# The second layer's first product as seven block products, tokens in two halves

## The chip, the cores and the metric

The kernel runs on one core of a Trainium2 chip. A core has five engines with queues of their own: TensorE (PE; its weight loads are listed apart as PEld), VectorE (DVE), ScalarE (ACT), GpSimd (POOL) and SyncE (SP, which here issues DMAs). Each engine works through its queue in program order and waits on semaphores for the others. SBUF is the working memory with 128 partitions; PSUM, eight banks of 128 x 512 float32, is where TensorE writes. The metric is the device time of one execution in microseconds (us).

## The reference

Three stages follow each other: clustered attention, a layer of eight experts of which each token takes one, and a layer of eight experts of which each token takes all, with weights from a balanced routing. The change lies in the third.

```python
def _moe2_ref(x, w_gate, w1, w2):            # x 1536 x 512, w1 8 x 512 x 1024, w2 8 x 1024 x 512
    logits = x @ w_gate
    logits = logits - logits.max()
    P = np.exp(logits)
    for _ in range(8):
        P /= P.sum(1, keepdims=True) + 1e-09
        P /= P.sum(0, keepdims=True) + 1e-09
        P *= N / E
    for e in range(E):
        h = np.maximum(x @ w1[e], 0.0)
        out += P[:, e:e + 1] * (h @ w2[e])
```

## The kernel before

All float32 products are made from two parts: a value rounded to the matmul's reduced format (`wh`, `xth`, `hh`; dtype fp32r) and the rest (`wl`, `xtl`, `hl`). A product of two such operands takes three matmuls: high by high, high by low, low by high. PSUM sums them.

Class `Weights` (L349 to L420) streams both layers' weights in chunks of 512 KB: 256 columns of `w1`, then the matching 256 rows of `w2`. `load` (L375) has SP issue the transfers into a ring of three raw buffers `wr`. `split` (L396 to L400) has ACT round a chunk into `wh` (L398) and DVE subtract to get `wl` (L399), then asks for later chunks. The parts stand in twelve slots. `get` keeps the split stream a fixed number of chunks ahead of use (`upto`).

First layer (loops at L821 on): per expert `e`, 256 token rows; per quarter `c` of the hidden dimension, `up` (L776 on) makes 24 matmuls of 256 columns into `hp` (L784), ACT and DVE make `hh` (L788) and `hl` (L789); `down` (L793 on) makes 12 matmuls of 512 columns into `acc` (L799), one quarter behind. After the last quarter, ACT and DVE copy `acc` to `y` (L802, L803) and SP writes it to the DRAM array `ys` (L808). `load2` (L723) reads 512 rows of `ys` back into `acc_o`; SP has to wait for the write to land first. `gated` (L729) multiplies a tile of 128 rows by its gate on DVE, and `rows` transposes it on TensorE (L738), after which ACT and DVE make `xth` and `xtl` (L740, L741). In the kernel before, `gated(0)` is issued eight quarters after its `load2`, four tiles are transposed at the end of the first layer, the other eight inside the second.

Second layer (loops at L957 on): per expert, three groups `g` of 512 tokens; per group eight slices `f` of 128 hidden columns. `up2` (L917 on) makes 12 matmuls of 512 columns into `hp` (L923), ACT makes `hh` (L926), DVE `hl` (L927). `down2` (L933 on) makes 12 matmuls of 512 columns into four `acc` banks (L937), one slice behind. After the eighth slice DVE scales `acc` by the routing weight `pm` and adds it to `acc_o` (L947); at the last expert POOL writes the rows out by an indirect DMA (L950). The second layer's routing, `balance` (L867 on), is threaded into the first slices: 24 matmuls for the logits (L877), then a chain of small DVE operations and small matmuls (L908).

The order on TensorE, ACT and DVE is that of the program text (a manual schedule); SP runs the DMA issues in one queue.

## Time and profile before

| | us |
|---|---|
| median of three runs | 1584.37 |
| lowest, highest | 1583.82, 1586.54 |
| span of the profiled execution | 1582.6 |
| TensorE busy in it | 1544.8 |
| DVE, ACT, POOL busy | 649.3, 497.7, 173.2 |
| second layer's first matmul starts at (timeline) | 497.60 |

The span runs from the first to the last instruction. The profiled execution's own device time is not listed apart from its span; the median of the runs is 1.8 us above the span, and that is taken for what lies around it. A matmul's listed duration overlaps the next one's, so what one costs is read from the distance of two starts, not from its duration.

### The profile page before, as it was taken

Reading aid. Unit: us, or ns where it says so; the run is one execution under the profiler, and the core shown is the slowest. Engines: PE = TensorE matmul, PEld = TensorE weight load, DVE = VectorE, ACT = ScalarE, POOL = GpSimd, SP = SyncE. Lnnn points to the kernel's source line nnn. Section 1 sums busy time; section 2 is a strip of 40 time slices with the busy share of each in tenths; the row PEclk is TensorE's granted clock in tenths of the full one; section 3 lists DMA queues with packets and bytes.
Section 4 is the critical chain, followed back from the end, with each engine's and each line's share of the span. In section 5 each row is a group of like instructions: output and inputs, shape, how many; then the busy total and the mean of one; then the engine's idle time right before and its main releaser. Section 6 shows DMA issues by size and latency. Waiting matters only on the chain.

```text
span 1582.6 us, 19864 instructions
## 1 busy us (share of the span) xinstructions
PE 1544.8 (98%) x7998; PEld 1306.0 (83%) x7998; DVE 649.3 (41%) x1109; ACT 497.7 (31%) x841; POOL 173.2 (11%) x205
## 2 busy tenths in 40 slices
PE   6999999799999999999999999999999999999998
PEld 5998999689998778888888888888888888888886
DVE  5888888556665225222411222231231132122111
ACT  3887778555554212211211211211121121111110
POOL 3254464132100000000000000000000000000000
PEclk9999999899999999999999999999999999999999
DMA  5575563286766001100200210120020021000000
GB/s 147 126 184 152 144 172 91 54 265 218 259 216 200 1 1 52 55 0 14 93 0 1 67 40 1 40 67 1 14 86 9 0 67 41 0 14 1 27 27 27
DMA packets 86591, 117.64 MB, mean 74 GB/s; under 512 B 20760, under 2 KB 55576, under 8 KB 86496
## 3 DMA queue, kind: packets, MB, share of 16 engines
q1 hardware_dynamic: 83216, 108.97, 23.5%
q0 software_dynamic: 2752, 7.36, 1.4%
q8 instruction: 64, 1.05, 0.3%
q14 instruction: 31, 0.25, 0.1%
q10 hardware_dynamic: 528, 0.02, 0.0%
HBM read 83.98 MB, written 10.51 MB: 60 GB/s over the span
## 4 chain that ended last, share of the span: by engine, by line
PE 76%; issue 2%; DMA 1%; DVE 1%; ACT 0%; POOL 0%; POOLq 0%; ACTq 0%
PE hp L923 33%; PE acc L937 32%; PE hp L784 5%; PE acc L799 5%; DMA wr<-w1a 1%; PE tp L771 0%; PE tp L877 0%; PE tp L738 0%; DVE wl L399 0%; DMA wr<-w2a 0%; ACT wh L398 0%; DMA xg<-xd,inv_i 0%; POOL out L950 0%; PE tp L908 0%; DVE hl L789 0%
## 5 line engine op out<-in xcount | busy, mean ns | idle before, releaser
L927 DVE SCALAR_TENSOR_TENSOR hl<-hp,hh 128x512 fp32r<-128x512 f32 x192 | 132.7, 691 | 743.6 <-ACT hh L926 743.5
L926 ACT ACTIVATE hh<-hp 128x512 fp32r<-128x512 f32 x192 | 115.0, 599 | 858.6 <-PE hp L923 858.6
L923 PE MATMUL hp<-xth,wh 128*128 128x512 f32 x768 | 305.4, 398 | 0.0
L923 PE MATMUL hp<-xth,wl 128*128 128x512 f32 x768 | 303.0, 394 | 0.0
L923 PE MATMUL hp<-xtl,wh 128*128 128x512 f32 x768 | 302.5, 394 | 0.0
L937 PE MATMUL acc<-wh,hh 128*128 128x512 f32 x768 | 301.7, 393 | 0.0
L937 PE MATMUL acc<-wl,hh 128*128 128x512 f32 x768 | 300.3, 391 | 0.0
L937 PE MATMUL acc<-wh,hl 128*128 128x512 f32 x768 | 300.0, 391 | 0.0
L923 PEld LDWEIGHTS hp<-xth,wl 128*128 128x128 f32 x768 | 144.1, 188 | 35.0
L937 PEld LDWEIGHTS acc<-wh,hl 128*128 128x128 f32 x768 | 144.2, 188 | 33.2 <-DVE hl L927 0.4
L937 PEld LDWEIGHTS acc<-wh,hh 128*128 128x128 f32 x768 | 144.2, 188 | 32.9 <-ACT hh L926 0.4
L923 PEld LDWEIGHTS hp<-xth,wh 128*128 128x128 f32 x768 | 144.3, 188 | 32.5
L923 PEld LDWEIGHTS hp<-xtl,wh 128*128 128x128 f32 x768 | 144.3, 188 | 32.4
L937 PEld LDWEIGHTS acc<-wl,hh 128*128 128x128 f32 x768 | 144.2, 188 | 32.2
L399 DVE TENSOR_TENSOR wl<-wr,wh 128x1024 fp32r<-128x1024 f32 x120 | 142.3, 1222 | 49.8 <-ACT wh L398 48.8
L398 ACT CAST wh<-wr 128x1024 fp32r<-128x1024 f32 x120 | 121.5, 1049 | 40.8 <-PE acc L799 20.4
L950 POOL DMA_INDIRECT out<-acc,tok x12 | 11.7, 975 | 1105.5 <-DVE acc L947 1068.1
L265 DVE TENSOR_TENSOR pl<-pst,ph 128x512 fp32r<-128x512 f32 x144 | 95.3, 680 | 12.1 <-ACT ph L261 12.1
L221 DVE TENSOR_REDUCE nm<-sp 128x1 f32<-128x768 f32 x96 | 91.0, 949 | 15.9 <-PE sp L212 15.2
L231 ACT ACTIVATE e<-sp,nm 128x768 f32<-128x768 f32 x96 | 86.9, 905 | 26.0 <-DVE nm L221 25.6
L261 ACT CAST ph<-pst 128x512 fp32r<-128x512 f32 x144 | 83.7, 585 | 26.3 <-PE pst L247 13.8
L277 PE MATMUL ov<-ph,v 128*128 128x256 f32 x288 | 80.6, 306 | 0.1
(213 smaller groups left out, 1865.4 us busy)
## 6 DMA issues: line engine op xcount, KB each, us to landing
wr<-w1a SPq DMA_DIRECT2D x32, 512.0 KB, 4.2
wr<-w2a SPq DMA_DIRECT2D x32, 512.0 KB, 4.5
wr<-w1b SPq DMA_DIRECT2D x32, 512.0 KB, 3.4
wr<-w2b SPq DMA_DIRECT2D x32, 512.0 KB, 4.2
q<-hh SPq DMA_DIRECT2D x32, 192.0 KB, 3.2
k<-hh SPq DMA_DIRECT2D x32, 192.0 KB, 3.6
ys<-y SPq DMA_DIRECT2D x8, 514.0 KB, 4.0
acc<-ys SPq DMA_DIRECT2D x3, 1028.0 KB, 7.0
```

The costliest lines, as they stand in the source:

```text
L221: nc.vector.tensor_reduce(out=nm, in_=sp[:, :, :384], axis=AX.XY, op=ALU.max, negate=True)
L231: nc.scalar.activation(out=e, in_=sp[:, :, :384], func=AF.Exp, bias=nm, accum_out=st["rs", t // 2][:, t % 2 : t % 2 + 1])
L261: nc.scalar.copy(out=w[3](w[1]), in_=w[0])
L265: nc.vector.tensor_tensor(out=w[3](w[2]), in0=w[0], in1=w[3](w[1].bitcast(F32)), op=ALU.subtract)
L277: nc.tensor.matmul(ov[:, :256], st["v2"][:, kt, :], w[:, kt, :], start=kt == 0 and i == 0, stop=kt == 5 and i == 1)
L398: self.nc.scalar.copy(out=wh, in_=r)
L399: self.nc.vector.tensor_tensor(out=wl, in0=r, in1=wh.bitcast(F32), op=ALU.subtract)
L784: nc.tensor.matmul(hp[:, f, :], w[:, kc, fs], xx[:, kc, :], start=kc == 0 and i == 0, stop=kc == 3 and i == 2)
L923: nc.tensor.matmul(hp, w[:, kc, fs], xx[:, kc, :], start=kc == 0 and i == 0, stop=kc == 3 and i == 2)
L926: nc.scalar.activation(out=hh, in_=hp, func=AF.Relu)
L927: nc.vector.scalar_tensor_tensor(out=hl, in0=hp, scalar=0.0, in1=hh.bitcast(F32), op0=ALU.max, op1=ALU.subtract)
L937: nc.tensor.matmul(acc[t], hx[:, as_], w[:, f % 2, :], start=f == 0 and i == 0, stop=f == 7 and i == 2)
```

## The change

The `w1` product of the second layer is made with seven block products in place of eight (Strassen, in Winograd's form). Tokens stand in two halves of 768. The work is cut in 64 items: half `s`, expert `e`, quarter `j` of the hidden dimension. In an item, x (768 tokens by 512) and `w1` (512 by 256) are cut 2 x 2; each block product is six matmuls of 384 columns, seven of them in an item make 42. The partial sums go through DVE (five additions), ACT (one copy, four roundings with relu) and DVE again (four low parts). The two PSUM banks `u0`, `u1` serve the seven groups in turn, and parts of the item before (`fill`, the 36 matmuls of 512 columns of its `w2` product) stand between the groups.

Weights are streamed once for each half. Each item's `w1` chunk is split twice: the chunk itself (`bh`, `bl`, of which three blocks are used) and, after four block subtractions in place, the four sums (`th`, `tl`). Slots go from twelve to nine, and `get` in the first layer runs 7 chunks ahead in place of 10. The block sums of the first half of x are built at the end of the first layer (`build_first`), those of the second half by POOL (item 8) and by ACT and DVE (item 31). `load2` reads six tiles after expert 4 and two tiles after experts 5, 6 and 7; ten of twelve tiles are gated and transposed in the first layer by a plan, and x keeps no split copy besides the block operands. The logits become 48 float32 matmuls of 8 columns with x as weights.

The core of the diff (renames, the same code moved, and the blocks' bookkeeping are cut):

```diff
 class Weights:
-    NA, NB = 8, 4
+    NS = 9
+        for _ in range(2):
             for e in range(8):
+                for j in range(4):
+                    self.src.append(w1b[e, j])
+                    self.src.append(w2b[e, j])
...
+    def build(self):
+        r = self.take()
+        th, tl = self.pair([128, 4, 256])
+        bh, bl = self.pair([128, 4, 256])
...
+        A.copy(out=bh, in_=r)
+        yield
+        for a in ((slice(0, 2), slice(0, 128)), (slice(2, 4), slice(0, 256))):
+            s_ = (slice(None),) + a
+            V.tensor_tensor(out=bl[s_], in0=r[s_], in1=bh.bitcast(F32)[s_], op=ALU.subtract)
+        yield
+        diff((0, 0), (0, 1), (0, 0))
+        diff((0, 1), (1, 1), (0, 1))
+        diff((1, 1), (1, 1), (0, 0))
+        diff((1, 0), (1, 0), (1, 1))
+        yield
+        A.copy(out=th, in_=r)
+        yield
+        V.tensor_tensor(out=tl, in0=r, in1=th.bitcast(F32), op=ALU.subtract)
+        self.load(3)
+        r = self.take()
+        wh, wl = self.pair([128, 2, 512])
+        A.copy(out=wh, in_=r)
+        yield
+        V.tensor_tensor(out=wl, in0=r, in1=wh.bitcast(F32), op=ALU.subtract)
+        self.load(3)
...
         def up(e, c, x):
-            wh, wl = W.get(0, e, c, 0, 2 * c + (8 if e == 0 else 10))
+            wh, wl = W.get(e, c, 0, 2 * c + 7)
...
-                if e in (3, 5):
-                    load2((e - 3) // 2)
+                if e == 4:
+                    load2(0, 6)
+                elif e > 4:
+                    load2(2 * e - 4, 2)
...
+        plan = {
+            (5, 1): "g0 g1", (5, 2): "r0 g2 r1 g3", (5, 3): "r2 g4 r3 g5 l0", (6, 0): "r4 r5 l2", (6, 1): "l4 g6 g7",
+            (6, 2): "r6 r7 x", (6, 3): "l6 x", (7, 0): "x x", (7, 1): "x g8 g9 w w", (7, 2): "x r8 r9 w w w", (7, 3): "l8 w",
+        }
...
+    GROUPS = (("a11", "b11", 0, True), ("s2", "t2", 1, True), ("a12", "b21", 0, False), ("s3", "t3", 1, False),
+              ("s1", "t1", 0, True), ("a22", "t4", 1, False), ("s4", "b22", 0, False))
...
+    def up2(k, fill, cuts, hooks):
+        wb = W.build() if k < 63 else iter(())
+        for g, (xn, wn, b, start) in enumerate(GROUPS):
+            for kc in range(2):
+                for i, (ww, xx) in enumerate(((wh, xh), (wh, xl), (wl, xh))):
+                    nc.tensor.matmul(p[:, N], ww[:, kc, :], xx[:, kc, :], start=start and kc == 0 and i == 0,
+                                     stop=kc == 1 and i == 2, skip_group_check=not start)
+            now = None
+            if g == 0:
+                r1 = new("r1")
+                nc.scalar.copy(out=r1, in_=p[:, N])
+            elif g == 1:
+                u2 = new("u2")
+                add(u2, r1, p)
+            elif g == 2:
+                nc.scalar.activation(out=parts("c11")[0], in_=p[:, N], func=AF.Relu)
+                lo("c11", p[:, N])
+            elif g == 3:
+                u3 = new("u3")
+                add(u3, r1, p)
+            else:
+                n, r = (("c22", u3), ("c21", r1), ("c12", u2))[g - 4]
+                c = new("cc", 2)
+                add(c, r, p)
+                nc.scalar.activation(out=parts(n)[0], in_=c, func=AF.Relu)
+                now = n, c
+            for f in hooks.get(g, ()):
+                f()
+            if g != 2:
+                next(wb, None)
+            if now:
+                lo(*now)
+            for f in fill[cuts[g] : cuts[g + 1]]:
+                f()
...
+    EVEN = [0, 5, 10, 15, 20, 25, 30, 36]
+    for k in range(64):
+        s, e, j = k // 32, k // 4 % 8, k % 4
+        cuts = EVEN
+        if k == 0:
+            cuts = [0, 12, 24, 24, 24, 24, 24, 24]
...
+        h = up2(k, fill, cuts, hooks)
+        fill = down2(s, e, j, h, acc, (3, 4, 5, 0, 1, 2) if k == 63 else None)
+    for f in fill:
+        f()
```

## Rows read from the trace of the kernel before

**Rows 1.** The page: busy us, share of the span and instructions by engine.

```profile
PE 1544.8 (98%) x7998; PEld 1306.0 (83%) x7998; DVE 649.3 (41%) x1109; ACT 497.7 (31%) x841; POOL 173.2 (11%) x205
```

**Rows 2.** The page's chain that ended last, shares of the span by line.

```profile
PE hp L923 33%; PE acc L937 32%; PE hp L784 5%; PE acc L799 5%; DMA wr<-w1a 1%; PE tp L771 0%; PE tp L877 0%; PE tp L738 0%; DVE wl L399 0%; DMA wr<-w2a 0%; ACT wh L398 0%; DMA xg<-xd,inv_i 0%; POOL out L950 0%; PE tp L908 0%; DVE hl L789 0%
```

**Rows 3.** Waits of PE from 297 us on: us in total, times, longest.

```profile
PE acc L799 <- ACT hh L788: 1.6, 1, 1.6
...
PE acc L799 <- DVE hl L789: 1.3, 2, 0.7
```

**Rows 4.** Busy time by engine, 640 to 1560 us: PE, PEld, DVE, ACT, POOL, clock, DMA.

```profile
640.00:1560.00 920.00, 920.00 (x3986) 747.92 (x3985) 227.62 (x305) 146.53 (x217) 7.82 (x8) 1.00 0.09 28
```

**Rows 5.** Chain in order of time, second layer, 16 slices: start us, us, what.

```profile
1350.69 2.80 PE hp L923 x12
...
1433.89 2.80 PE hp L923 x12
```

**Rows 6.** The same chain, end of the first layer.

```profile
489.42 2.87 PE hp L784 x24
492.30 5.47 PE acc L799 x24
```

**Rows 7.** Timeline of PE in the attention: start us, us, line, tile, shape.

```profile
152.57 0.34 PE L210 MATMUL sp<-k,q 96*128 96x384 f32 x1
...
153.29 0.38 PE L254 MATMUL pst<-ident,e 128*128 128x128 f32 x2
```

**Rows 8.** Groups of instructions: shapes, count, busy us, mean ns, idle before.

```profile
L784 PEld LDWEIGHTS hp<-xh,wh 128*128 128x128 f32 x256 | 49.7, 194 | 1.3 <-ACT xh L773 0.5
```

**Rows 9.** Groups of DVE and ACT, the same columns.

```profile
L399 DVE TENSOR_TENSOR wl<-wr,wh 128x1024 fp32r<-128x1024 f32 x120 | 142.3, 1222 | 49.8 <-ACT wh L398 48.8
L927 DVE SCALAR_TENSOR_TENSOR hl<-hp,hh 128x512 fp32r<-128x512 f32 x192 | 132.7, 691 | 743.6 <-ACT hh L926 743.5
...
L947 DVE SCALAR_TENSOR_TENSOR acc<-acc,pm,acc 128x512 f32<-128x512 f32 x84 | 58.2, 744 | 3.8 <-PE acc L937 2.5
...
L293 DVE TENSOR_TENSOR x_sb<-pst,rr 128x144 f32<-128x144 f32 x48 | 14.2, 296 | 2.8 <-PE pst L290 2.8
...
L398 ACT CAST wh<-wr 128x1024 fp32r<-128x1024 f32 x120 | 121.5, 1049 | 40.8 <-PE acc L799 20.4 <-DMA wr<-w1a 14.3 <-DMA wr<-w2a 4.0
L926 ACT ACTIVATE hh<-hp 128x512 fp32r<-128x512 f32 x192 | 115.0, 599 | 858.6 <-PE hp L923 858.6
...
L286 ACT COPY ot<-ov 128x256 f32<-128x256 f32 x48 | 17.9, 372 | 3.5 <-PE ov L277 2.2
```

**Rows 10.** Timeline of SP after experts 3 and 4; then DMA issues, KB each, us to landing.

```profile
407.20 0.39 SPq L808 DMA_DIRECT2D ys<-y  x1
...
410.74 0.37 SPq L723 DMA_DIRECT2D acc<-ys  x1
...
430.57 0.39 SPq L808 DMA_DIRECT2D ys<-y  x1
...
wr<-w1a SPq DMA_DIRECT2D x32, 512.0 KB, 4.2
...
acc<-ys SPq DMA_DIRECT2D x3, 1028.0 KB, 7.0
```

**Rows 11.** Chain, quarters 0 and 3 of expert 5 in the first layer.

```profile
424.10 2.87 PE hp L784 x24
...
441.83 2.87 PE hp L784 x24
```

**Rows 12.** Waits from 295 to 345 us, the first layer's start.

```profile
ACT wh L398 <- DMA wr<-w1a: 9.0, 5, 5.1
```

**Rows 13.** Timeline of PE: twelve float32 products with 128 x 128 weights.

```profile
158.36 1.42 PE L164 MATMUL pst<-c,qk 128*128 128x32 f32 x12
159.62 0.41 PE L254 MATMUL pst<-ident,e 128*128 128x128 f32 x2
```

More of the change, by code (lines that the diff above doesn't have):

```diff
@@ L739, in rows, with logits @@
-        ts_ = slice(128 * (t % 4), 128 * (t % 4) + 128)
-        nc.scalar.copy(out=xth[g][:, :, ts_], in_=tp)
-        nc.vector.tensor_tensor(out=xtl[g][:, :, ts_], in0=tp, in1=xth[g].bitcast(F32)[:, :, ts_], op=ALU.subtract)
+        xg = row(t)
+        tp = ps3.tile([128, 512], F32, name="tp")
+        for kc in range(4):
+            ks = slice(128 * kc, 128 * kc + 128)
+            nc.tensor.transpose(tp[:, ks], xg[:, ks], ident)
+        nc.scalar.copy(out=xg[:, 0:512], in_=tp)
+    def logits(t0, n):
+        lp = ps3.tile([128, 2, 8], F32, name="tp")
+        for t in range(n):
+            for kc in range(4):
+                nc.tensor.matmul(lp[:, t, :], row(t0 + t)[:, 128 * kc : 128 * kc + 128], wgr[:, kc, :],
+                                 start=kc == 0, stop=kc == 3)
+        nc.vector.tensor_copy(out=l2[:, t0 : t0 + n, :], in_=lp[:, 0:n, :])
@@ L793, in down, with mm, end @@
         def down(e, c, h, acc, y):
[L794 to L801 removed]
+            wh, wl = W.get(e, c, 1)
+            def mm(f, a, i, hx, w):
+                nc.tensor.matmul(acc[a], hx[:, f, 128 * a : 128 * a + 128], w[:, f, :],
+                                 start=c == 0 and f == 0 and i == 0, stop=c == 3 and f == 1 and i == 2)
+            def end():
                 nc.scalar.copy(out=y[:, 0, 0:512], in_=acc[0])
@@ L913, in balance @@
             nc.vector.tensor_tensor(out=pm, in0=pm, in1=cs.unsqueeze(1).to_broadcast([128, 12, 8]), op=ALU.mult)
+        yield
     bal = balance()
[L917 to L929 removed]
@@ L931, in tile_kernel, with routing @@
-    put = []
-    def down2(e, g, f, h, acc, t):
-        wh, wl = W.get(1, e, f // 2, 1)
-        as_ = slice(128 * t, 128 * t + 128)
-        for i, (hx, w) in enumerate(((h[0], wh), (h[0], wl), (h[1], wh))):
-            nc.tensor.matmul(acc[t], hx[:, as_], w[:, f % 2, :], start=f == 0 and i == 0, stop=f == 7 and i == 2)
-        if f < 7:
-            return
-        tt = 4 * g + t
-        ao = acc_o[g][:, t, 0:512]
+    next(bal)
+    def routing(ps):
+        try:
+            bal.send(ps)
+        except StopIteration:
+            pass
@@ new lines, in build_second @@
+    def build_second():
+        raw = {n: xblock(1, n) for n in ("a11", "a12", "a21", "a22")}
+        for o, a, b, op in (("s3", "a11", "a21", ALU.subtract), ("s1", "a21", "a22", ALU.add),
+                            ("s2", "s1", "a11", ALU.subtract), ("s4", "a12", "s2", ALU.subtract)):
+            raw[o] = raw["a21"] if o == "s1" else view(sp.tile([128, 2, 384], F32, name=f"r{o}"))
+            nc.gpsimd.tensor_tensor(out=raw[o], in0=raw[a], in1=raw[b], op=op)
+        yield
+        last = None
+        for n in XN + (None,):
+            if n:
+                h, l = xo[1][n] = xtiles(n)
+                nc.scalar.copy(out=view(h), in_=raw[n])
+            if last:
+                nc.vector.tensor_tensor(out=view(last[1]), in0=last[2], in1=view(last[0].bitcast(F32)), op=ALU.subtract)
+            last = n and (h, l, raw[n])
+            yield
@@ new lines, in tile_kernel, with bank, parts, lo @@
+    HB = dict(c11=1, c12=1, c22=2, c21=2)
+    GROUPS = (("a11", "b11", 0, True), ("s2", "t2", 1, True), ("a12", "b21", 0, False), ("s3", "t3", 1, False),
+              ("s1", "t1", 0, True), ("a22", "t4", 1, False), ("s4", "b22", 0, False))
+    N = slice(0, 384)
+    banks = {}
+    def bank(k):
+        if k not in banks:
+            banks[k] = ps1.tile([128, 512], F32, name="hp", tag=f"u{k}")
+        return banks[k]
+    def up2(k, fill, cuts, hooks):
+        s = k // 32
+        w = W.items[k][0]
+        ps = [bank(k % 2), bank(1 - k % 2)]
+        h = {}
+        tmp = {}
+        wb = W.build() if k < 63 else iter(())
+        add = lambda o, a, p: nc.vector.tensor_tensor(out=o, in0=a, in1=p[:, N], op=ALU.add)
+        new = lambda n, b=1: t2.tile([128, 384], F32, name=n, bufs=b)
+        def parts(n):
+            h[n] = [h2.tile([128, 384], F32R, name=f"{n}{i}", bufs=HB[n]) for i in range(2)]
+            return h[n]
+        def lo(n, src):
+            nc.vector.scalar_tensor_tensor(out=h[n][1], in0=src, scalar=0.0, in1=h[n][0].bitcast(F32),
+                                           op0=ALU.max, op1=ALU.subtract)
+        late = None
+        for g, (xn, wn, b, start) in enumerate(GROUPS):
+            p = ps[b]
+            xh, xl = xo[s][xn]
+            wh, wl = w[wn]
+            for kc in range(2):
[15 more added lines that the diff above has]
+                add(u3, r1, p)
+            else:
+                n, r = (("c22", u3), ("c21", r1), ("c12", u2))[g - 4]
[3 more added lines that the diff above has]
+                now = n, c
+            if g == 6:
+                del banks[k % 2], banks[1 - k % 2]
+            for f in hooks.get(g, ()):
[6 more added lines that the diff above has]
+                f()
+        for _ in wb:
+            pass
+        return h
```

318 lines of the change are left out of this document (184 added, 134 removed).

## The prediction

> **What bounds the kernel now.** I read the page's busy times first: TensorE 1544.8 us of 1582.6, every other engine under half [rows 1]. A reader should not stop there, since matmul durations overlap. The chain that ended last says the same in another way: two lines, the second layer's two products, carry 65% of the span [rows 2]. Then the waits of TensorE: from 297 us on, its longest are 1.6 and 1.3 us [rows 3]. So from there on it is fed, and the busy table of 640 to 1560 us has it busy for all 920 us at full clock while DVE has work for 228, ACT for 147, and the DMA engines for 9% at 28 GB/s [rows 4]. TensorE's columns are the limit, and the other engines have room there. What the change is worth is thus columns removed, times the price of a column, less any wait that the new work of DVE and ACT puts before TensorE.
>
> **What a product costs now.** Starts of the `hp` groups, 15 slices from 1350.69 to 1433.89, give 83.20 / 15 = 5.547 us for a slice of 12 + 12 matmuls; the first twelve take 2.80, which leaves 2.75, or 0.229 each, for L937 [rows 5]. There are 8 x 3 x 8 = 192 slices: 1065.0 us.
>
> **What it costs afterwards.** An item has 42 matmuls of 384 columns and 36 of 512; there are 64. No product of 384 columns stands in the layers' code, so its price is bounded. From below: in the first layer 24 products of 256 columns take 492.30 - 489.42 = 2.88 us, 0.120 each, and 24 of 512 take 5.47, 0.228 each [rows 6]; the middle is 0.174. From above: four products of 384 columns in the attention (L210 and L212 in turn) take 153.29 - 152.57 = 0.72, 0.180 each [rows 7]. Both are about as near, so I take 0.177. The products of 512 columns keep 0.229 [rows 5]; I take 0.230 with 0.231 as upper end, for the changed order. An item is 42 x 0.177 + 36 x 0.230 = 7.43 + 8.28 = 15.71, and 64 of them 1005.7. That saves 59.3 us. The ends: 0.174 and 0.229 give 995.5 (69.5 saved), 0.180 and 0.231 give 1016.1 (48.9 saved). The count alone, 42 x 384 against 48 x 384 columns, leaves no doubt that the work shrinks by an eighth of the first product.
>
> **What lies beside it: DVE and ACT.** DVE's durations go with length: 144 elements 0.296, 512 0.691, 1024 1.222 [rows 9]; on that line 256 cost 0.42, 384 0.55, 768 0.96. One item asks of DVE: low parts of the weights 0.42 + 0.69 + 1.22 + 1.22, four block subtractions 1.66, five sums out of PSUM 2.77, four low parts 2.22, and of the accumulator's six evictions per four items (0.744 each) 1.12. Together 11.3 of 15.7 us. ACT: three roundings of 1.049 and five steps of 384 at about 0.49 (256 cost 0.372, 512 0.599): 5.6 us. Both fit as sums. Does each piece fit in time? A PSUM bank is written again two groups later, so its reader has one other group and two fills: 6 x 0.177 + 10 x 0.230 = 3.36 us. The longest queue ahead of a reader is at group 4: after group 3 ends DVE does a sum (0.55) and four block subtractions (1.66), done 2.2 us later, just when group 4 ends (1.06 + 1.15); its sum takes 0.55 more. Slack 2.8 us. After group 5, sum, `tl` and a low part (2.3 us) fill the 2.2 us to group 6's end, and the last low part of the item is wanted some 12 fills and three groups later, 5.9 us, against 0.6 + 0.5 + 1.2 + 0.6. The routing's ten steps add about nine small DVE operations each in items 2 to 6, inside the same slack, and put as much on TensorE as before. So I cost DVE and ACT at nothing; the cover is those fills. Without them it would be the second rival's price.
>
> **Weights twice.** 32 MB more over some 1000 us takes the stretch from 28 to about 60 GB/s [rows 4]; a chunk of 4.2 us [rows 10] is wanted each 7.8 us. Nothing.
>
> **The first layer's start.** TensorE's 2.9 us of waits [rows 3] are where ACT has roundings queued, ahead of `hh`, that wait for chunks (9.0 us in five waits, [rows 12]). Looking ahead 7 chunks in place of 10 means that `hh` sits behind chunks that were asked for earlier. I take -2.5, between -2.9 and 0.
>
> **Tiles read back earlier.** This is an added wait. After expert 4 SP writes `y` at 430.57 (one expert after 407.20), may read back only when that landed, 3.5 us later, and 1028 KB take 7.0 us [rows 10]. At (7.0 - 4.2) per further 512 KB the new 1542 KB take 9.8, so they land near 443.9. DVE meets `g0` at the end of quarter 1 and stands there, with `g1`, two weight splits and `hl` behind it. TensorE meets `r0` when quarter 2 ends, at 441.83 [rows 11], and goes on about 0.5 after landing: +2.6 (0 to 5). The two-tile reads after experts 5 and 6 (3.5 + 4.2 after their write) are met a quarter later than they land, by a margin of some 1.5 us. They cost nothing, but would cost what the write is late beyond that. SP stands for those 3.5 us with weight issues behind it, as it does now after expert 3, without a TensorE wait.
>
> **The seam.** Item 0 has a fill behind group 0 only. From group 1 to 6 TensorE needs 6 x 1.06 = 6.4 us; DVE up to the sum that frees the next item's bank has 6.1 us that start 1.3 after group 1: about +1 (0 to 4). **Item 31** also builds the second half's operands: 7 x 0.96 = 6.7 more for DVE, 2.3 over the item's time, nearly all inside the slack: +0.5 (0 to 2.3). **Logits:** 24 x 0.230 = 5.5 go, 48 float32 products of 8 columns come at no more than the 1.26 / 12 = 0.105 of those with 32 columns [rows 13], 5.0: -0.5 (-3 to 0). The transposes only move between layers. **The end** keeps its shape, six matmuls for a tile, then DVE and POOL: 0.
>
> **Sum.** -59.3 - 2.5 + 2.6 + 1 + 0.5 - 0.5 = -58.2 against the profiled execution's span of 1582.6: 1524.4. With the 1.8 us by which the median of the runs, 1584.37, stands above that span: 1526. All low ends give 1509, all high ends 1547; not all come together, so the forecast's own range is 1512 to 1546.
>
> **Rivals.** *The weight load sets the pace.* Each product loads 128 x 128 weights, listed at 0.194 us [rows 8], and 384 columns stream in less. If a load could not be hidden behind a shorter product, the 42 would cost 0.194 each: an item 16.43, in all 1051.5, 13.5 saved, 1572. Against it: products of 256 columns follow each other at 0.120 with the same 0.194 loads between them [rows 6, 8], so loads run beside each other and beside matmuls. 4%. The Trainium skill (TensorE: Matmul & The Clock Gate, The mechanism) says that a weight load overlaps a running matmul only if the two use different row groups, which full 128-row loads here never do; by it the loads would stand in the way as in this rival. The trace disagrees: 0.120 is less than the load alone.
>
> *DVE sets the pace.* If its instructions on blocks or out of PSUM cost half as much again as on the line above, an item takes 11.3 x 1.5 = 17.0 us of DVE, TensorE waits for banks in each item, and 64 x 17.0 = 1088 is 23 more than now: about 1607, slower. It decides from 1065 / 64 = 16.6 us an item, a surcharge of 47%. Against it: the measured durations of both sources lie on one line [rows 9]. 4%.
>
> *Banks come late now and then.* The queue order costs 0.3 to 0.8 us an item, at a place that I counted as slack: 64 x 0.5 = 32, 1558. For it: TensorE never waits now, so no row shows the new chain, with an ACT step between two DVE steps. Against it: the 2.8 us of slack. 8%.
>
> **How the numbers follow.** Forecast 82%, the three rivals 4, 4 and 8, and 2 for a mix of the last two that eats the gain. A measurement of this kernel can tell about 0.2%, 3 us, from no change. Forecast, first and third rival are faster, 0.94; the mix is the same, 0.02; the second rival slower, 0.04. 1512 to 1546 holds all but a few of the forecast's cases and leaves the rivals out: 8 in 10.
>
> **What would show it.** Right: starts of the 384-column products 0.174 to 0.180 apart, items 15.6 to 15.9 apart, no TensorE wait for `hp` banks beyond a few us in all, DVE near 70% in the second layer, one wait of about 3 us for the first transposes near 442 us, none near 324 and 336. Wrong: a pitch of 0.19 or more, or a wait for DVE in every item; or waits of many us at the seam, where the read-back of the last two tiles (asked for in item 0, used in item 1) is the thing I trust least.

## The result: 1540.0 us, 0.972 of the time before

| | before | after |
|---|---|---|
| median of the runs, us | 1584.09 (1582.65 to 1586.54) | 1540.01 (1538.60 to 1541.53) |
| ratio | | 0.9723, 95% interval 0.9709 to 0.9737 |
| span of the profiled execution | 1582.6 | 1538.8 |

The time lies in the forecast's range and 14 us above its value. The page of the changed kernel, busy times and granted clock (compare [rows 1]); the last line is the clock row of the kernel before:

```profile
PE 1492.8 (97%) x8442; PEld 1357.5 (88%) x8442; DVE 1058.3 (69%) x1952; ACT 672.6 (44%) x1107; POOL 179.3 (12%) x209
PEclk9999999899989999999999999999999999999999
...
PEclk9999999899999999999999999999999999999999
```

TensorE still carries the span, and DVE went from 649 to 1058 us without becoming the bound. The clock row is new in one place: slice 12 (423 to 462 us) is below full. Slice 8 (270 to 308 us) is so in both. The middle of the second layer, in the busy table (columns as in [rows 4]):

```profile
1060.00:1520.00 460.00, 460.00 (x2299) 415.74 (x2298) 300.96 (x532) 159.65 (x239) 0.00 (x0) 1.00 0.19 63
```

TensorE is busy in all of it at the full clock, DVE in 65%, and the weights come at 63 GB/s where it was 28 before. One item there, read from the timeline (start, duration, engine, line, operation): the first product of each of the seven groups, and that of the next item.

```profile
726.96 0.51 PE L1144 MATMUL hp<-a,wh 128*128 128x384 f32 x2
728.01 0.40 PE L1097 MATMUL acc<-wh,c 128*128 128x512 f32 x1
729.15 0.51 PE L1144 MATMUL hp<-s,wh 128*128 128x384 f32 x2
731.36 0.51 PE L1144 MATMUL hp<-a,wh 128*128 128x384 f32 x2
733.55 0.51 PE L1144 MATMUL hp<-s,wh 128*128 128x384 f32 x2
735.75 0.51 PE L1144 MATMUL hp<-s,wh 128*128 128x384 f32 x2
737.96 0.51 PE L1144 MATMUL hp<-a,wh 128*128 128x384 f32 x2
740.15 0.51 PE L1144 MATMUL hp<-s,wh 128*128 128x384 f32 x2
742.58 0.51 PE L1144 MATMUL hp<-a,wh 128*128 128x384 f32 x2
```

Six products of 384 columns take 728.01 - 726.96 = 1.05 us, 0.1755 each; five of 512 take 1.14 to 1.15, 0.229 each; the item takes 742.58 - 726.96 = 15.62, and 15.627 as a mean of many.

Cut at two points that both traces have, the time went here. The sum's terms are put to the stretch that they belong to; of the logits, five of six blocks lie in the second stretch, and the transposes of six more tiles (0.4 each) move into it from the third.

| stretch | before | after | change | by the sum |
|---|---|---|---|---|
| to quarter (5,1) of the first layer | 429.55 | 425.07 | -4.5 | -2.5 |
| from there to the second layer's first product | 68.0 | 89.5 | +21.5 | +9.2 |
| second layer | 1085.0 | 1024.2 | -60.8 | -64.9 |
| span | 1582.6 | 1538.8 | -43.8 | -58.2 |

So the gain of the steady items arrived, and more: 64 x 15.627 = 1000.1 in place of 1005.7. What is missing was lost at the end of the first layer (12.3 us against the sum) and in the first items of the second (4.1 + 5.6 = 9.7 against it). Of these, 2.75 us only cross the cut: the last twelve products of 512 columns of the first layer stand ahead of the second layer's first product in the kernel before (the 24 at 492.30 in [rows 6]), and behind item 0's first group in the changed one:

```profile
515.69 0.40 PE L929 MATMUL acc<-wh,hh 128*128 128x512 f32 x1
```

For the same work on both sides the losses are thus 15.0 and 7.0. TensorE's waits there are small; most of the loss is TensorE at work, at half its clock or on more instructions than were counted. The end of the first layer in the timeline:

```profile
440.79 1.94 PE L805 MATMUL tp<-ident,acc 128*128 128x128 f32 x8 [3.63 <-DVE acc L797]
442.38 0.56 PE L915 MATMUL hp<-xh,wh 128*128 128x256 f32 x1
442.74 0.41 PE L915 MATMUL hp<-xh,wl 128*128 128x256 f32 x1
442.96 0.41 PE L915 MATMUL hp<-xl,wh 128*128 128x256 f32 x1
...
450.03 1.03 PE L805 MATMUL tp<-ident,acc 128*128 128x128 f32 x8
451.30 1.95 PE L812 MATMUL tp<-wgr,acc 128*128 128x8 f32 x16 [0.24 <-ACT acc L806]
453.11 0.36 PE L915 MATMUL hp<-xh,wh 128*128 128x256 f32 x1
...
453.90 0.42 PE L915 MATMUL hp<-xl,wh 128*128 128x256 f32 x1
454.11 0.41 PE L915 MATMUL hp<-xh,wh 128*128 128x256 f32 x1
```

Three things are to be seen. The one wait that was forecast is there, 3.63 us for the first tile that was read back. Behind it, products of 256 columns start 0.21 us apart (442.74, 442.96) where they started 0.12 apart in [rows 6]: the granted clock is 0.50 there, the lower of the two levels, 1.2 GHz in place of 2.4. And the logits of two tiles, eight products, are listed as 16 instructions that take 453.11 - 451.30 = 1.81 us; half a microsecond behind them, with TensorE idle for no more than the 0.24 us ahead of them, the clock is at the lower level again, for most of a group. The busy table by quarter says the same in its clock column (the one before the last two):

```profile
442.70:453.20 10.50, 10.26 (x62) 9.48 (x61) 6.05 (x13) 5.71 (x8) 0.00 (x0) 0.80 0.61 200
453.20:463.50 10.30, 10.06 (x62) 9.28 (x62) 3.82 (x5) 4.18 (x7) 0.00 (x0) 0.83 0.45 153
463.50:474.80 11.30, 10.34 (x62) 9.55 (x62) 4.42 (x6) 3.96 (x6) 2.47 (x2) 0.82 0.41 142
474.80:489.80 15.00, 15.00 (x97) 13.96 (x98) 7.00 (x11) 7.30 (x10) 0.00 (x0) 0.91 0.33 106
```

And TensorE's waits from item 0 to item 6 (engine, line waited at, releaser: total, times, longest):

```profile
PE hp L1144 <- DVE c L1134: 2.1, 1, 2.1
PE hp L1144 <- DVE cs L1029: 1.8, 4, 0.5
PE hp L1013 <- DVE m L1012: 0.8, 1, 0.8
PE hp L1144 <- DVE cc L1126: 0.7, 1, 0.7
```

These 5.4 us are the seam (2.1), the routing (1.8 and 0.8) and a sum that came late (0.7). Items 2 to 6 take 17.23, 16.74, 16.80, 16.84 and 16.83 us in place of 15.63.

### The profile page after: what moved, and what is told of

Read it like the earlier page. It is cut to its first block, busy times and chain, and to the rows that moved or that the text cites. A ratio compares the mean times of both kernels' runs of the same rounds, so it can differ in the third digit from the quotient of the medians.

```text
span 1538.8 us, 22218 instructions
## 1 busy us (share of the span) xinstructions
PE 1492.8 (97%) x8442; PEld 1357.5 (88%) x8442; DVE 1058.3 (69%) x1952; ACT 672.6 (44%) x1107; POOL 179.3 (12%) x209
## 4 chain that ended last, share of the span: by engine, by line
PE 41%; issue 32%; DVE 4%; DMA 2%; POOL 1%; ACT 1%; POOLq 0%; ACTq 0%; DVEq 0%; SPq 0%
PE hp L1144 14%; PE acc L1097 10%; PE hp L915 5%; PE acc L929 5%; PE tp L1097 5%; DVE wr L453 1%; PE tp L812 1%; DMA acc<-ys 1%; POOL out L1080 1%; DMA wr<-w2a 1%; DVE cc L1126 0%; DMA ys<-y 0%; DVE c L1134 0%; DVE wl L468 0%; PE tp L805 0%
## 5 line engine op out<-in xcount | busy, mean ns | idle before, releaser
L1097 PE MATMUL acc<-wh,c 128*128 128x512 f32 x1024 | 350.0, 393 | 0.0
L1144 PE MATMUL hp<-s,wh 128*128 128x384 f32 x1024 | 264.0, 339 | 3.0 <-DVE c L1134 2.1
L1097 PEld LDWEIGHTS acc<-wh,c 128*128 128x128 f32 x1024 | 191.7, 188 | 28.4
L1144 PEld LDWEIGHTS hp<-s,wh 128*128 128x128 f32 x1024 | 188.8, 188 | 24.3 <-DVE c L1134 2.5
L1097 PE MATMUL acc<-wl,c 128*128 128x512 f32 x512 | 200.8, 392 | 0.0
L1144 PE MATMUL hp<-a,wh 128*128 128x384 f32 x768 | 198.0, 339 | 1.8 <-DVE cs L1029 1.8
L1097 PE MATMUL tp<-wh,c 128*128 128x512 f32 x512 | 180.2, 393 | 0.0
L1144 PE MATMUL hp<-s,wl 128*128 128x384 f32 x512 | 172.9, 338 | 0.0
L1144 PEld LDWEIGHTS hp<-a,wh 128*128 128x128 f32 x768 | 141.6, 188 | 17.8 <-ACT wh L472 2.6
L1144 PE MATMUL hp<-a,wl 128*128 128x384 f32 x384 | 129.8, 338 | 0.0
```

What stands on the lines that cost most here:

```text
L1097: nc.tensor.matmul(acc[t], hx[:, 128 * (t % 3) : 128 * (t % 3) + 128], w_[:, f if t < 3 else 1 - f, :], start=j == 0 and f == 0 and i == 0 ...
L1144: nc.tensor.matmul(p[:, N], ww[:, kc, :], xx[:, kc, :], start=start and kc == 0 and i == 0, stop=kc == 1 and i == 2, skip_group_check=not ...
```

## The experiments

The theory at this point: the steady items go at TensorE's own pace; the rest of the forecast was lost to the lower clock behind narrow work, to a wait for memory at the seam (where the first layer's end meets item 0), and to the routing. Each experiment has its rival, stated with what was expected. Spans are compared stage by stage, since executions differ by up to 7 us before quarter (5,1) begins (it starts between 420.1 and 427.3 us in kernels that are the same up to there).

### Who sets the pace of an item

**e6_eight.** Group 6 is issued twice, which makes the work of eight block products with the side work of seven (the sum that it feeds is then another).

```diff
+            if g == 6:
+                for kc in range(2):
+                    for i, (ww, xx) in enumerate(((wh, xh), (wh, xl), (wl, xh))):
+                        nc.tensor.matmul(p[:, N], ww[:, kc, :], xx[:, kc, :], start=False,
+                                         stop=kc == 1 and i == 2, skip_group_check=True)
```

> Group 6 of each item is done twice, an eighth block product's worth of work (six products of 384 columns; the sum is then wrong). All the rest stays. Theory, TensorE alone sets the pace: each item takes 6 x 0.176 = 1.05 us more, 16.68, the span 1538.8 + 67.5 = 1606, slower than the kernel before. Rival, part of the steady pace is set by DVE or by the banks: the longer item gives slack and less than 60 us are added.

Measured: 1607.1 us. Two item starts in the timeline:

```profile
1206.78 0.51 PE L1144 MATMUL hp<-a,wh 128*128 128x384 f32 x2
1223.46 0.51 PE L1144 MATMUL hp<-a,wh 128*128 128x384 f32 x2
```

16.68, which is 1.05 more: six products at 0.1755, nothing hidden and nothing added. An eighth product costs its columns. With all the block sums and the second stream of weights, but without the seventh saved, the kernel would be 23 us slower than before: the saving of columns is the whole of the gain, and it pays for the side stages.

**e7_dve.** The two largest subtractions of each item, `tl` and `wl`, are done twice, some 2.3 us more of DVE in each item.

```diff
         V.tensor_tensor(out=tl, in0=r, in1=th.bitcast(F32), op=ALU.subtract)
+        V.tensor_tensor(out=tl, in0=r, in1=th.bitcast(F32), op=ALU.subtract)
...
         V.tensor_tensor(out=wl, in0=r, in1=wh.bitcast(F32), op=ALU.subtract)
+        V.tensor_tensor(out=wl, in0=r, in1=wh.bitcast(F32), op=ALU.subtract)
```

> Each item does the subtractions for tl and wl twice: 2.3 us of DVE more per item, some 13.2 of 15.63. Theory, DVE's work lies under TensorE's and the fills cover its queue: items keep 15.63 us, the span stays within 3 us of 1538.8 (items 2 to 8 with routing and extra scalings may lose 0.5 each). Rival, DVE is near its limit by the order of its queue: TensorE waits for banks in each item, 0.3 us or more each, 1558 or more.

Measured: 1550.9 us, with the steady items unchanged at 15.63. The busy table of the middle:

```profile
1060.00:1500.00 440.00, 440.00 (x2198) 397.61 (x2197) 356.92 (x571) 155.05 (x232) 0.00 (x0) 1.00 0.20 68
```

And TensorE's longest waits from 500 to 660 us, items 0 to 9:

```profile
PE hp L1146 <- DVE cs L1031: 6.9, 4, 1.7
PE hp L1146 <- DVE c L1136: 2.6, 1, 2.6
```

DVE at 357 of 440 us, 81%, does not hold TensorE once in this stretch. The 11 us, where at most 3 were expected, came elsewhere: items 2 to 6 take 17.8 to 18.1, item 9 18.7, items 32 and 33 16.1 and 16.3, and the seam 1.6 more. The cover that the forecast named is real, and the places that have little of it are those where the change lost time.

### The end of the first layer

**e1_nolog.** The logits are left out (the routing then works from zeros); the transposes stay.

```diff
     def logits(t0, n):
+        return
```

> The logits of the second layer (48 float32 products of 8 columns, 96 instructions) are left out; the routing weights then come from zeros, so the output differs. Theory, narrow work lowers TensorE's clock: the span falls from 1538.8 by six times about 1.7 us of the products, 1.4 us of waits ahead of them, and about 4.6 us because the groups of 24 products of 256 columns that follow them at 453, 464 and 475 us take 2.83 us again in place of 4.46, 4.47 and 4.21: about 1523. Rival, the transposes ahead of the logits lower the clock: the three groups still take over 4 us, and only the products and waits go: about 1527.

Measured: 1518.5 us. From quarter (5,1) to item 0 it takes 73.1 us (420.50 to 493.56) where the changed kernel takes 89.5. The groups behind transposes take 2.8 to 2.9, at full clock; only the one behind the wait for the read-back (4.32 here) is slow, 4.12. The clock column where it was 0.82 above:

```profile
450.00:463.00 13.00, 13.00 (x91) 11.83 (x91) 6.32 (x12) 7.74 (x11) 1.90 (x2) 1.00 0.77 243
463.00:476.00 13.00, 13.00 (x86) 11.79 (x85) 10.68 (x12) 8.71 (x12) 0.00 (x0) 1.00 0.58 176
```

So leaving out the logits gave 16.4 us in this stretch, of which 5 x 1.7 = 8.5 are the instructions themselves; transposes without logits behind them do not lower the clock. The other 8 are the clock behind the logits (4.6), the waits for PSUM buffers that they share with the transposes (2.8), and 0.5 that the read-back's wait and its slow group came out shorter in this execution.

**e2_spread.** The logits' products are woven one by one between the 512-column products of the next quarter.

```diff
+        for i, f in enumerate(fs):
+            r.append(f)
+            if i < len(ls):
+                r.append(ls[i])
```

> The logits' products of the first layer stay, but stand one at a time between the 512-column products of the next quarter in place of sixteen instructions in a row. Theory, a row of narrow products lowers the clock: the three groups at 453, 464 and 475 us take 2.83 us again (-4.6) and the waits ahead of the logits go (-1.4), the products themselves cost the same 1.7 us a time: about 1533. Rival, the transposes are the cause: no change of the groups, 1537 to 1539. A third: each switch between a narrow and a wide product costs about 0.1 us, 40 of them +4: about 1537 with the groups at 2.83.

Measured: 1536.4 us; from (5,1) to item 0 81.2 us, 8.2 less, and the up groups of the quarters behind logits at 2.91 or less. Twelve 512-column products with eight logits among them take 4.57 where twelve alone take 2.75, so the narrow products cost the same 1.8 for two tiles as in a row. It is not their number that the clock answers to. (Of the 8.2, 1.7 only moved: the last two tiles' logits now stand among item 0's fills, and item 0 takes 15.81 in place of 14.11. Up to item 2 it is 6.5 less; the span fell by 4.2 only, since that execution reached (5,1) 2.2 us later.)

Nor is it a row of them alone. In the traces of the eight kernels that keep the rows, a row with no transposes directly ahead is followed by the full clock in all 25 cases. A row directly behind transposes, with the waits for PSUM buffers that come with it, is followed by a slow group (4.2 to 5.3) in 20 of 23. One of the other three, in e3_late, below:

```profile
460.96 1.26 PE L805 MATMUL tp<-ident,acc 128*128 128x128 f32 x8 [0.96 <-DVE xl L905]
462.29 1.95 PE L812 MATMUL tp<-wgr,acc 128*128 128x8 f32 x16
464.10 0.36 PE L915 MATMUL hp<-xh,wh 128*128 128x256 f32 x1
```

The group that starts at 464.10 takes 2.91. So weaving helps because it breaks up a stretch of transposes and logits; which part of that stretch the clock falls for, and why it does not in three cases, stays open.

**e3_late.** The tiles are gated and transposed a quarter later.

```diff
-            (5, 1): "g0 g1", (5, 2): "r0 g2 r1 g3", (5, 3): "r2 g4 r3 g5 l0", (6, 0): "r4 r5 l2", (6, 1): "l4 g6 g7",
-            (6, 2): "r6 r7 x",
+            (5, 2): "g0 g1", (5, 3): "r0 g2 r1 g3", (6, 0): "r2 g4 r3 g5 l0", (6, 1): "r4 r5 l2 g6 g7",
+            (6, 2): "l4 r6 r7 x",
```

> The first six tiles are gated and transposed one quarter later. Theory, TensorE's 3.6 us wait at 440.8 us is the read-back of expert 4, and the half clock behind it is its consequence: the wait goes (-3.6), eight transposes take 0.87 in place of 1.59 us (-0.7 or more), the group behind them 2.83 in place of 4.71 (-1.9): about 1532.5. Rival, the work queued on DVE is late anyway: the wait moves to the next transposes and 1 us or less is gained: 1538.

Measured: 1530.3 us; from (5,1) to item 0 79.8, 9.7 less. The wait is gone and no longer lowers the clock; one group is still slow (4.44, behind the logits at 449.97). So the wait of 3.63 cost more than itself: the transposes and the group behind it at the lower clock made it 6.5 (3.63 + 0.8 + 2.07). Two of the three slow groups behind logits are gone too, some 3 us, which accounts for the rest: one of these two rows now has no transposes directly ahead, the other is the one at 462.29.

### The seam

The changed kernel's ACT waits there for something that is no operand (waits of ACT, 514 to 535 us):

```profile
ACT c L1154 <- DMA ys<-y: 4.2, 1, 4.2
```

TensorE's timeline behind it:

```profile
523.88 0.62 PE L1144 MATMUL hp<-s,wh 128*128 128x384 f32 x2 [2.15 <-DVE c L1134]
...
525.78 0.84 PE L1144 MATMUL hp<-a,wh 128*128 128x384 f32 x2
526.42 0.52 PE L1144 MATMUL hp<-a,wl 128*128 128x384 f32 x1
```

The tile `c11` lies in SBUF where the closed pool of `y` lay, and `y` is being written out by a DMA. ACT stands, DVE's `lo` stands behind it, TensorE waits 2.15 for the bank and then does ten products of 384 columns at 0.32 each (525.46 to 528.66), the lower clock level again.

**e4_seam.** The pool of `y` is opened first, so that another part of the second layer's memory follows it.

```diff
-        hp_ = st.enter_context(tc.tile_pool(name="hp", bufs=3))
         yp = st.enter_context(tc.tile_pool(name="yp", bufs=2))
+        hp_ = st.enter_context(tc.tile_pool(name="hp", bufs=3))
```

> The pool of the first layer's y buffers is opened first, so that their memory is used again by the second half's block sums and not by item 0's c11. Theory, at the seam ACT waits 4.2 us for the write of y out of memory that c11 takes over, TensorE waits 2.15 us behind it and then runs 18 products at half clock (0.32 in place of 0.176 each, 2.6 us): both go, 1538.8 falls to about 1534. Rival, my forecast's reason, DVE has more to do in item 0 than TensorE: a wait of about 1 us at another group stays and 1534 to 1538 comes out, with the clock down as now.

Measured: 1537.9 us; from item 0 to item 2 31.20 in place of 33.46. ACT's wait, TensorE's 2.15 and the low clock are gone; what is left at the seam are two waits for DVE's sums, 0.33 and 0.38 (waits from 514 to 531 us in e4_seam):

```profile
PE hp L1144 <- DVE cc L1126: 0.7, 2, 0.4
```

The backlog that the forecast counted as 1 us is 0.7. But the first layer's 512-column products now take 2.80 for twelve in place of 2.755.

### The routing

**e5_route.** The second of the item's two routing steps is moved from behind group 6 to behind group 5.

```diff
-            hooks[6] = [lambda k=k: routing(bank(1 - k % 2)[:, 384:512])]
+            hooks[5] = [lambda k=k: routing(bank(1 - k % 2)[:, 384:512])]
```

> The second of an item's two routing steps (items 2 to 6) stands after group 5 in the bank that group 5 has done with, in place of after group 6 in the next item's first bank. Items 2 to 6 take 16.7 to 17.2 us now, 15.63 later on. Theory, the next item's first group waits for the small DVE operations that read the routing's part of its bank: 0.46 us of wait and the restart go in each item, items 3 to 6 take about 16.2, span 1536.5. Rival, the two float32 products of a step and their place between wide ones cost the 1.2 us: no change, 1538.8.

Measured: 1545.4 us, slower; items 2 to 6 take 17.9, 19.9, 19.9, 18.3 and 19.9. TensorE's waits there:

```profile
PE hp L1028 <- DVE cc L1126: 7.9, 4, 2.0
```

The step's product now waits 2 us each time for DVE's sum out of the bank that it writes to, which itself stands in DVE's queue behind the rest of group 4; behind three of these four waits the clock falls. Neither theory nor rival had this: the place of the step decides not by the slack behind it but by which bank it borrows and what DVE still has to do with that bank.

**e10_noroute, e12_noroute_pad.** The routing's steps are left out (the weights are a constant), and GpSimd's four sums for the second half are held back from item 1 to item 10. (The program text has them at item 8, but GpSimd ran them from 535.96 us on, in item 1.) The second of the two kernels also has three unused tiles in place of the routing's small ones, so that the tiles behind them in SBUF lie where they lie in the changed kernel (by the expectation's reckoning; the traces show no addresses).

```diff
     def routing(ps):
+        return
...
+            if o == "s3":
+                nc.vector.memset(raw[o][:, 0, 0, 0:1], 0.0)
...
-        if k == 8:
+        if k == 10:
             hooks[0] = [lambda: next(bs)]
```

> The changed kernel without the routing's steps in items 2 to 6 (the routing weights are a constant, so this part of the computation is left out), and with GpSimd's sums held back to item 10. Theory: items 2 to 6 are 1.2 us longer than the steady 15.63 because of the routing's small products, which wait for DVE there: without them these five items take 15.6 to 15.7 and the time falls by 6 us; the four block subtractions of item 0 or 1 that took 5.74 us beside GpSimd's sums take 1.8, and TensorE's wait of 0.74 at 545.5 is gone. Span near 1532. Rival 1: the items are long because the second layer's weight stream or DVE is still behind after the seam: they stay at 16.5 or more and the span at 1538. Rival 2: the block subtractions are slow for a reason of their own in item 0: they stay above 4 us for the four with GpSimd silent.

> The changed kernel without the routing's steps (left out; the routing weights are a constant) and with GpSimd's sums at item 10, once more, but with three unused tiles in the place of the routing's three small ones, so that hh, hl and the second layer's h tiles lie where they lie in the changed kernel (96 modulo 128; at 0 in the run before). Theory of placement: 512-column products go from 0.234 back to 0.229 in both layers, items from 15.73 to 15.63, and the span falls by 64 x 0.1 + 32 x 0.05 = 8 us against that run, to about 1533; items 2 to 6 stay at the steady 15.63. Rival: the wider pitch came from the routing being absent (another stream of instructions) or from that execution: it stays, span near 1542.

Measured: 1543.8 and 1527.3 us. Items 2 to 6 of the first are as long as its steady ones, 15.73, and of the second 15.63. The starts of items 3 and 4 in the second:

```profile
556.78 0.34 PE L1150 MATMUL hp<-a,wh 128*128 128x384 f32 x1
572.41 0.51 PE L1150 MATMUL hp<-a,wh 128*128 128x384 f32 x2
```

From item 2 to item 62 it takes 938.3 us where the changed kernel takes 944.7: the routing costs 6.4 us, shown. That the time of the first kernel rose all the same is in part the placement, below: from item 2 to item 62 its wider pitch takes back 5.9 of the 6.4. The first layer's end took 3.3 more in that execution, and (5,1) came 1.2 later. In both, DVE's four block subtractions that had stood beside GpSimd's sums are back at 0.42 each (the line's group: count, then min, median and max of one in ns). The changed kernel, 515 to 560 us:

```profile
L453 DVE TENSOR_TENSOR wr<-wr x12: 402/424/1854, 524.2 to 558.5; 128x256 f32<-128x256 f32 x12
```

The first kernel without routing, the same stretch:

```profile
L453 DVE TENSOR_TENSOR wr<-wr x11: 415/425/427, 514.7 to 559.7; 128x256 f32<-128x256 f32 x11
```

In the changed kernel four of them took 5.74 us (from 539.22) while GpSimd did its sums of 1.6 to 1.8 us each (538.79 to 544.22), and TensorE waited 0.74 behind that. The Trainium skill (SBUF — State Buffer, SBUF: two separate sides) says that a VectorE operation with two SBUF inputs and a GpSimd operation that reads SBUF exclude each other for a whole instruction. By that rule, the trace agrees: the slowest subtraction, 1.85, is as long as one of GpSimd's sums. Held back to item 10, the sums slow two other subtractions with both inputs in SBUF, 2.9 us from start to end where the pair takes 1.02 elsewhere; the sums of DVE that read PSUM stay at 0.55 beside them. In e9_best, 666 to 676 us:

```profile
L459 DVE TENSOR_TENSOR wl<-wr,wh x2: 925/1480/2036, 670.0 to 670.8; 128x256 fp32r<-128x256 f32 x1, 128x512 fp32r<-128x512 f32 x1
```

### All together

**e8_all** has the edits of e2, e3, e4 and e5; **e9_best** those of e2, e3 and e4 and the held-back sums of GpSimd.

> Four of the edits together: spread logits, tiles one quarter later, the y pool first, routing after group 5. If each theory holds and the gains add: -6.0 - 6.3 - 4.7 - 2.3 = -19 on the span, about 1520, the time about 1521, 4% below the kernel before. Rivals: gains overlap (one clock recovery counted twice): 1525 to 1530; or the waits move on: 1535.

> The three edits of the first layer's end and the seam together (logits' products woven singly between the next quarter's products, tiles a quarter later, the y pool opened first), the routing left as in the changed kernel, and GpSimd's four sums of the second half held back to item 10 by a one-column write of DVE to their first target. Theory: the kernel with all edits lost its gain only to the moved routing steps: from item 2 to item 62 it took 956.1 us where the changed kernel takes 944.7. Without that, its span of 1537.6 becomes 1526.2, and the held-back sums give back the 0.7 us wait at 545.5: a span near 1525.5, a time near 1527, items 2 to 6 at 16.8 and from (5,1) to item 0 76 us. Rival: the stages do not add up, because a later stage gives the time back (the wider pitch of the first layer's 512-column products in the kernel with the y pool first, 1.4 us in all, and an earlier item 0 that waits longer for its last tiles): a span of 1530 or more.

Measured: e8_all 1539.4 us (1538.0 to 1539.8), ratio 0.9725 (0.9698 to 0.9752), no better than the changed kernel: 13.0 us won up to item 0 and 0.5 at the seam, 11.4 lost again from item 2 on to the moved routing step, and 1.0 by a later quarter (5,1) in that execution. e9_best 1526.4 us (1522.9 to 1526.7), ratio 0.9635 (0.9620 to 0.9650), span 1524.7: from (5,1) to item 0 76.4 in place of 89.5, from item 0 to item 2 31.9 in place of 33.5, the rest the same. In both kernels 1.7 of the 13.0 are the logits that moved into item 0. The stages add up to the span, as its expectation had it, but the edits' own gains do not: up to item 2 e2, e3, e4 and the held-back sums won 6.5, 10.0, 4.1 and (in e12) 1.0, but together 14.6, in part because e2 and e3 remove two of the same slow groups. And the clock stays: three stretches of the first layer's end, whose clock was 0.80 to 0.91,

```profile
453.00:463.00 10.00, 9.03 (x66) 8.06 (x65) 4.91 (x11) 4.32 (x8) 1.91 (x2) 1.00 0.57 182
463.00:475.00 12.00, 12.00 (x89) 11.18 (x88) 5.35 (x7) 7.05 (x10) 0.00 (x0) 1.00 0.28 90
475.00:490.00 15.00, 15.00 (x101) 13.65 (x101) 11.07 (x15) 4.20 (x6) 0.00 (x0) 1.00 0.56 177
```

With e11_pad, below, it is the fastest kernel here that leaves no work out, 0.9% faster than the changed one.

### Where a tile lies

In e4, e8, e9 and e10 products of 512 columns take longer, in e10 in both layers (0.233 in place of 0.230 in the second; those of 384 stay at 0.175). **e11_pad** is e9_best with 64 unused bytes per partition ahead of `hp`.

```diff
+        yp.tile([128, 16], F32, name="ypad", bufs=1)
         hp_ = st.enter_context(tc.tile_pool(name="hp", bufs=3))
```

> The kernel with the first layer's and the seam's edits and the routing as changed, and 64 unused bytes per partition ahead of the hp pool, so that hh and hl start at the same byte modulo 128 (96) as in the changed kernel; nothing else differs. Theory: the 512-column products of the first layer run 0.233 apart (2.80 for twelve) in the kernels with the y pool first, and 0.229 (2.755) in the others, because of where hh and hl lie in SBUF (there modulo 128 at 32, here at 96): the pitch goes back to 0.229, 32 quarters give back 32 x 0.045 = 1.4 us, a time near 1525. Rival: the pitch belongs to the order in which the pools are opened or to the chip, and stays at 0.233: 1526.4.

Measured: 1526.4 us (1524.8 to 1527.8), the same as e9_best. Twelve products of 512 columns take 2.78 to 2.80 in place of 2.80, and 24 of 256 take 2.85 in place of 2.82: the theory, that it is the start of `hh` and `hl` modulo 128 bytes, falls. The pair e10 and e12 stands: two kernels with one stream of work but for three small writes of GpSimd, the tiles shifted by 96 bytes, and twelve products of 512 columns at 2.80 against 2.755, items at 15.73 against 15.63. It is not the chip either, since e9_best ran on the same one as e10 with items of 15.63. So the pitch depends on where operands lie in SBUF, as far as one execution of each of the two can show it; by which rule is open. In this kernel it is worth up to 64 x 0.1 + 32 x 0.05 = 8 us, an estimate.

## Why the prediction was right, and where it was off

**The products, right.** Pitch 0.1755 and 0.229 where 0.177 and 0.230 were taken: 64.9 us saved where the sum has 59.3. The nearer of the two bounds was the lower one, from the first layer's products [rows 6]. The rival of the weight load is out: each of these products loads weights, listed at 0.188 on average, and they start 0.1755 apart. A group of these loads on the page (count, busy us, mean ns):

```profile
L1144 PEld LDWEIGHTS hp<-s,wh 128*128 128x128 f32 x1024 | 188.8, 188 | 24.3 <-DVE c L1134 2.5
```

**DVE beside it, right in the steady items.** It is busy 65% there, and 81% would do (e7). Two rivals fall with it, DVE as the pace and banks that come late now and then: there is no wait at all from item 10 to item 63. Before that banks do come late, in items 0, 1 and 3 to 6. **Weights twice** cost nothing, as the sum has it, at 63 GB/s.

**The routing, wrong by 4.1 us.** The step that failed is "The routing's ten steps add about nine small DVE operations each in items 2 to 6, inside the same slack". The slack was worked out for group 4 and for the low parts, not for the bank that the step borrows: the second step's small product sits in the bank that the next item writes first, six fills later, and DVE reads it only behind a weight split, a low part and a sum. So TensorE waits 0.46 at the end of each of items 3 to 6:

```profile
581.97 0.42 PE L1144 MATMUL hp<-a,wh 128*128 128x384 f32 x1 [0.46 <-DVE cs L1029]
```

From start to start that wait and the restart cost 0.7; the small products, and the slower first product behind each, make up the other 0.5 of the 1.2 us an item. The cover named was the fills; here there were six of them, 1.4 us, against DVE's 2. e6 shows the same from the other side: with six more products in the last group this wait is gone, and items 3 to 6 are 0.45 longer than the steady ones (17.13 against 16.68), not 1.2. The routing costs 6.4 in all; the kernel before paid 2.3 for its own, ten slices of 57.76 us in place of 55.47, from the first of these lines to the second:

```profile
566.73 0.50 PE L923 MATMUL hp<-xth,wh 128*128 128x512 f32 x1
...
624.49 0.49 PE L923 MATMUL hp<-xth,wh 128*128 128x512 f32 x1
```

**The logits, mis-sized twice.** The row taken for the price [rows 13] counts instructions, and a float32 product is listed as two of them: the eight products of two tiles are x16. At 0.106 per instruction the price was right and the number half: 48 products take 96 instructions, 10.2 us, not 5.0. And the clock falls for the group that follows three of the rows, which no row of before could show, since its logits had 512 columns: three groups at 4.44, 4.45 and 4.20 in place of 2.83 are 4.6 us more. e1 and e2 show that they come with the rows of logits; that transposes directly ahead are needed too is seen in the traces alone.

**The read-back, right in kind.** The reading took 9.74 us by the chain of waits, 9.8 in the sum; the write 4.0 in place of 3.5. TensorE waited 3.63 where the sum has 2.6. What is missing is the price behind a wait: the group that followed at the lower clock took 4.90 in place of 2.83, the transposes 1.59 in place of 0.79, 2.9 us in all. Nor was that new: in the kernel before, the waits of [rows 3] at 336 us stand in a stretch (332 to 343 us) whose granted clock is 0.84, and the quarter that begins at 332 us took 10.5 us there; without those waits it takes 6.4 after the change.

That is also why **the first layer's start** gave 4.5 in place of 2.5: the waits at 336 us went with the low clock behind them, while those near 324 us stayed (0.7 and 0.6), where the prediction's signs had none. (The 1.3 us in [rows 3], read as a longest wait, are two, the longest 0.7.) Since single executions differ by up to 7 us at this point, the size is not settled.

**The seam, right in size of its own step and wrong in what comes first.** DVE's backlog costs 0.7 (1 in the sum), in e4, where nothing stands ahead of it. But in the changed kernel a reused piece of SBUF, still being read by a DMA, held ACT for 4.2 us ahead of it, and TensorE lost 2.15 and some 1.5 at the low clock. Item 0 takes 14.11 where its products alone take 10.1, and the range for this step, 0 to 4, just holds that; the reason is another. **Item 31** cost nothing (15.63), 0.5 in the sum. Item 9, where the accumulator is scaled once more (L1076), takes 16.13: 0.5 that the sum does not have.

The account, in us against the sum:

| where | terms | together |
|---|---|---|
| products | 64.9 saved, 59.3 in the sum | -5.6 |
| start of the first layer | 4.5 in place of 2.5 | -2.0 |
| end of the first layer | logits 4.9, the clock behind them 4.6, the wait 1.0 and the clock behind it 2.9, transposes held up by PSUM buffers 2.2, less the 2.75 of products that moved behind item 0's first group (0.5 too much, of which eleven quarters of 5.59 in place of 5.62 are 0.3) | +12.3 |
| second layer | the same 2.75, routing 4.1, seam and late sum 4.2 (5.2, with 1 in the sum), logits 0.9, items 7 to 9 0.7, less 0.5 for item 31, less 1.9 for the old logits (7.4 with their transposes and a wait, 5.5 in the sum), less about 1 at the kernel's end (0.5 stays open) | +9.7 |

Together this is +14.4, and 1524.4 + 14.4 is the span of 1538.8.

So the mechanism of the gain is right, and that the total stayed inside 1512 to 1546 is in part luck. The read-back with the clock behind it (6.5 against 0 to 5), the logits (a cost where -3 to 0 was given) and the routing (4.1 against nothing) lie outside what was allowed for them, and the products' 5.6 and the start's 2.0 made up for a third of the rest.

## What to carry to other kernels

A change that takes columns from a TensorE-bound loop pays what the columns cost; what decides the rest is the few places without cover: the first items, a borrowed bank, the join of two stages. There, follow each small step through the queue of the engine that must release its bank or its memory, also memory of a pool just closed. Price a TensorE wait with the slow group behind it, not by its own length; keep transposes and narrow products from standing together in one stretch, put the narrow ones singly between wide ones; and count instructions, not products, in a row of the profile.

## What was new about the hardware

- Eight products of 8 columns in a row (16 instructions, 1.8 to 2.3 us) directly behind transposes are followed by TensorE at 1.2 GHz for most of a group in 20 of 23 cases, 0.213 us for 256 columns in place of 0.12, although it is idle for 0.24 us at most in two of three cases in the changed kernel. The same 16 instructions singly between 512-column products are not (e2), and neither are transposes of 128 columns in a row without logits behind them or a wait ahead of them (e1).
- Rows of logits without transposes directly ahead of them are not either, in 25 of 25 cases; the next group takes 2.91 (the changed kernel at 487.96).
- Another place of the tiles in SBUF changes the pitch of 512-column products from 0.230 to 0.233 (e12, e10; one execution each).
- A DVE subtraction of 0.42 us with both inputs in SBUF takes up to 1.85 beside a GpSimd sum; a DVE sum that reads PSUM stays at 0.55 (e9).
